# Turning the kept blocks one step earlier, and moving the side tasks into the fresh unit's split

## The chip, the cores and the metric

The kernel runs on one core of one Trainium2 chip. The metric is the device time of one execution in microseconds (us). TensorE is written PE (PEld is its weight load), VectorE DVE, ScalarE ACT; SP is SyncE, which here issues nearly all DMAs. The kernel before took 2707.97 us (median of three runs, 2707.35 to 2708.66).

## What is computed

Three layers follow each other over 4 batches of 3072 rows with 256 columns (12288 rows in all). The reference, cut to its core:

```python
scores = np.matmul(z, z.transpose(0, 2, 1)) / S      # z: 4 x 3072 x 64, symmetric scores
x = u * np.matmul(np.maximum(scores, 0.0) ** 2, v)   # attention without softmax
h = x @ w_in                                         # 256 -> 2048
x = (h - np.tanh(h)) @ w_out                         # 2048 -> 256
xk = mu_k * x + (1 - mu_k) * x_prev                  # x_prev: the row above, zero at a batch's start
xr = mu_r * x + (1 - mu_r) * x_prev
k = np.maximum(xk @ w_k, 0.0)                        # 256 -> 1024
out = 1 / (1 + np.exp(-(xr @ w_r))) * ((k * k) @ w_v)
```

Weights arrive in float64 and are made float32 in the kernel.

## The kernel before

**Tiles.** Rows are cut into 24 tiles of 512 (`t` or `i`), six (`NG`) to a batch; `g = t % 6` is a tile's place in its batch. Everything is held transposed, with columns on the partitions and 512 rows along the free dimension. Each product is made of three matmuls (`PASSES`): each operand is split into a high part (`h`) and the rest (`l`), and high by high, high by low and low by high are summed. So every intermediate goes from PSUM through an ACT function, is copied to `h` and has `l = a - h` taken from it on DVE (`sub_lo`, line 96) before PE can use it.

**Units.** The work is a list of 504 units, `units`, which the loop at line 702 takes one by one as `n`. A unit's `produce` issues its first matmuls and its split, and `consume` of the unit two places back (`LAG` = 2) issues the matmuls that add it to the accumulator. A unit `A` (12 for each of 24 tiles) is a 256 x 512 block of the squared scores, `H` (8 a tile) a 256-column slice of the tanh layer, `K` (4) one of the squared layer, `R` (1) the sigmoid. All `A` units come first; behind them `H` of a tile is interleaved with `K` and `R` of the tile before.

**Fresh and re-read units.** Scores are symmetric, so a block of tile pair (i, g) that was made for tile i is, transposed, also a block for tile g. In tiles g = 1 to 5, blocks of source tiles i below `min(g, 3)` (`AGAIN` = 3) are not made again: they were stored to DRAM when fresh (`keep`), are loaded as tiles `b` by SP seven units ahead (`again_load`) and turned by DVE (line 401). A fresh unit has 4 + 12 matmuls, and ACT does relu (line 339), square (340) and, for g above 1, the copy to `h` (93). A re-read unit has 12 matmuls alone; DVE does two transposes, ACT the copy to `h_t` (93), DVE `l_t` (96). `pairs[g]` sets the order of a tile's units. For g = 3 to 5 it is re-read, fresh, re-read, fresh and so on, six of each.

**Order.** Engines run their instructions in the order in which the code is written; nothing is rearranged. For unit n the loop runs: DMA loads due (`loads`), the store of the unit before, `produce(n)`, `consume(n - 2)`, `turned_high(n + 1)` (if unit n+1 is re-read: its two transposes and the copy to `h_t`), and `run_steps(n)`. When a re-read unit is produced, only `l_t` is left to do. `run_steps` places side tasks: the z, v, u and weight preparation of later tiles, the product with `u` that ends a tile (`x1_steps`), and in the last stage the mixing with the row above (`mix_steps`) and the output. Each has a first place, a last place and a cost per step. A unit has a budget (line 677 to 680: 1.4 for A with g up to 1; 2.1 for fresh and 0.1 for re-read units with g above 1; 2.2 for H, 2.4 K, 4.0 R), and up to 1.0 of an unused budget is carried to the next unit (`spare`, line 689), as is any overdraft.

**Buffers.** Score and tanh results have two PSUM tiles (`wk`), accumulators two (`acc`), `h` and `l` three each, ACT's results (`a_`, `t_`, `g_`) four (`scratch`), the re-read blocks share twelve with v and the weights.

Of the kernel before, what the change touches and what calls it, by code (L numbers as in the profile page):

```python
# [19 lines left out]
def relu2_attention__tanh_ffn__channel_mix_kernel(  # L20
# [25 lines left out]
    nc = tc.nc  # L46
# [6 lines left out]
    NT = B * NG  # L53
# [4 lines left out]
    LAG = 2  # L58
# [33 lines left out]
    def copy_hi(o, i):  # L92
        nc.scalar.activation(out=o, in_=i, func=ACTF.Copy)  # L93
# [232 lines left out]
    def parts(name):  # L326
        h = sb.tile([P, 2, 512], F32R, tag="hi", name=f"h_{name}", bufs=3)
        l = sb.tile([P, 2, 512], F32R, tag="lo", name=f"l_{name}", bufs=3)
        return h, l
# [1 line left out]
    def scratch(name):  # L331
        return sb.tile([P, 2, 512], F32, tag="e", name=name, bufs=4)

    def square_split(name, w, sc, pieces=1, high=nc.vector.tensor_copy):
        a = scratch(f"a_{name}")
        h, l = parts(name)
        for j in range(pieces):
            x = slice(2 * j // pieces, 2 * (j + 1) // pieces)
            nc.scalar.activation(out=a[:, x], in_=w[:, x], func=ACTF.Relu, scale=sc)  # L339
            nc.scalar.activation(out=a[:, x], in_=a[:, x], func=ACTF.Square)  # L340
            high(h[:, x], a[:, x])  # L341
            sub_lo(l[:, x], a[:, x], h[:, x])
        return a, h, l
# [5 lines left out]
    for g in range(NG):  # L349
        of_f = [2 * j + h for j in fresh[g] for h in range(2)]  # L350
        of_r = [2 * j + h for j in again[g] for h in range(2)]
        if g == 1:
            of_f = of_f[2:] + of_f[:2]
        if len(of_r) == 2:
            pairs[g] = of_f[:8] + [of_r[0], of_f[8], of_r[1], of_f[9]]
        elif len(of_r) == 4:
            pairs[g] = [x for i in range(4) for x in (*of_f[2 * i : 2 * i + 2], of_r[i])]
        elif of_r:
            pairs[g] = [x for i in range(6) for x in (of_r[i], of_f[i])]
        else:  # L360
            pairs[g] = of_f
    kept = {(b, i, g): dr.tile([TB, TB], F32, name=f"at{b}_{i}_{g}")
# [18 lines left out]
        g, q = n // NP % NG, n % NP  # L381
        return pairs[g][q] // 2 in again[g]

    def turned_high(n):
        if not is_again(n):
            return
        t, q = divmod(n, NP)
        b, g = divmod(t, NG)
        kp = pairs[g][q]
        x = blocks[b, g, kp // 2]  # L390
        a = scratch(f"t_{t}_{q}")
        h, l = parts(f"t_{t}_{q}")
        for j in range(2):
            f = kp % 2 * 2 + j
            y = x[:, :, f * 32 : f * 32 + 32]
            if g < AGAIN:
                y = y.rearrange("p (c k) i -> p k c i", c=4)
                o = a[:, j].rearrange("p (k c i) -> p k c i", k=4, c=4)
            else:
                o = a[:, j].rearrange("p (m i) -> p m i", i=32)  # L400
            nc.vector.transpose(out=o, in_=y)  # L401
        copy_hi(h, a)
        turned[n] = (a, h, l)

    def produce(unit):
        kind, t, p = unit
        name = f"{kind}{t}_{p}"
        n = at[unit]
        if n in turned:
            a, h, l = turned.pop(n)  # L410
            sub_lo(l, a, h)
            split[unit] = (h, l)
            return
        w = work(f"w_{name}")
        if kind == "A":
            b, g = divmod(t, NG)
            kp = pairs[g][p]
            for j in range(2):
                kc = 2 * kp + j
                lhsT = z1[b, kc // 4][:, (kc % 4) * P : (kc % 4 + 1) * P]  # L420
                nc.tensor.matmul(w[:, j], lhsT, zq[b, g], start=True, stop=False)  # L421
                nc.tensor.matmul(w[:, j], lhsT, z2[t], start=False, stop=True)  # L422
            a, *split[unit] = square_split(
                name, w, scale, 2 if t == 0 and p == 0 else 1,
                copy_hi if g > 1 else nc.vector.tensor_copy,
            )
            if (b, g, kp // 2) in kept:
                stores[n + 1] = lambda: keep(b, g, kp, a)
        elif kind in ("H", "K"):
            wt = "in" if kind == "H" else "k"  # L430
            x = xs[t] if kind == "H" else mixed["k", t]
            for j in range(2):
                f = 2 * p + j
                n = 0
                for c in range(DC):
                    for a, m in PASSES:
                        nc.tensor.matmul(  # L437
                            w[:, j],
                            ws[wt, f // 4][a][:, c, (f % 4) * P : (f % 4 + 1) * P],
                            x[m][:, c],  # L440
                            start=n == 0,
                            stop=n == 3 * DC - 1,
                        )
                        n += 1
            if kind == "K":
                _, *split[unit] = square_split(name, w, 1.0)
            else:
                g = scratch(f"g_{name}")
                h, l = parts(name)
                nc.scalar.activation(out=g, in_=w, func=ACTF.Tanh)  # L450
                nc.vector.tensor_tensor(out=g, in0=w, in1=g, op=ALU.subtract)  # L451
                copy_hi(h, g)
                sub_lo(l, g, h)
                split[unit] = (h, l)
        elif kind == "R":
            x = mixed["r", t]
            for d in range(DC):
                n = 0
                for c in range(DC):
                    for a, m in PASSES:  # L460
                        nc.tensor.matmul(  # L461
                            w[:, d],
                            ws["r", 0][a][:, c, d * P : (d + 1) * P],
                            x[m][:, c],
                            start=n == 0,
                            stop=n == 3 * DC - 1,
                        )
                        n += 1
            s = p4(f"sg{t}")
            nc.scalar.activation(out=s, in_=w, func=ACTF.Sigmoid)  # L470
            split[unit] = s
# [135 lines left out]
    def task(first, last, steps, *args):  # L607
        tasks.append([last, first, len(tasks), steps, args])
# [9 lines left out]
    for t in range(NT):  # L618
        load(t * NP - NP + 1 if t > 1 else 5 + 3 * t, u_load, t)
        task(t * NP - 6 if t > 1 else 8 + 3 * t, t * NP + NP - 2, u_steps, t)  # L620
        if t:
            load(t * NP - 3, z_swap, t)
        task(t * NP + NP + LAG - 1, t * NP + NP + LAG + 3, x1_steps, t)
    for b in range(1, B):
        prev = (b - 1) * NG * NP
        last = prev + (NG - 1) * NP
# [43 lines left out]
    def run_steps(n):  # L670

        for x in [x for x in tasks if x[1] <= n]:
            tasks.remove(x)
            ready.append((x[0], list(x[3](*x[4]))))
        ready.sort(key=lambda x: x[0])
        kind = units[min(n, len(units) - 1)][0]
        left = {"A": 1.4, "H": 2.2, "K": 2.4, "R": 4.0}[kind]
        if kind == "A" and n // NP % NG > 1:
            left = 0.1 if is_again(n) else 2.1
        left += spare[0]  # L680
        while ready and (left > 0 or ready[0][0] <= n):
            for x in list(ready):
                if left > 0 or x[0] <= n:
                    cost, f = x[1].pop(0)
                    f()
                    left -= cost
                    if not x[1]:
                        ready.remove(x)
        spare[0] = min(left, 1.0)

    with tc.manual_schedule():
        z_load(0, 0)
        z_load(0, 1)
        v_load(0, 0)
        z_load(0, 2)
        v_load(0, 1)
        for cost, f in z_steps(0, 0) + z_steps(0, 1) + v_steps(0, 0):
            f()
        for m, src in ((0, moe2_mu_k), (1, moe2_mu_r)):
            with nc.allow_non_contiguous_dma(reason="a column of the mixing vector"):  # L700
                nc.sync.dma_start(out=mu[:, m, :], in_=src.rearrange("(c p) -> p c", p=P))
        for n in range(len(units) + LAG + 3):
            for f in loads.pop(n, ()):
                f()
            if n in stores:
                stores.pop(n)()
            if n < len(units):
                produce(units[n])
            if LAG <= n < len(units) + LAG:
                consume(units[n - LAG])  # L710
            turned_high(n + 1)
            if n == 1:
                nc.vector.memset(zero, 0.0)
                nc.vector.tensor_scalar(
                    out=omu, in0=mu, scalar1=-1.0, scalar2=1.0, op0=ALU.mult, op1=ALU.add
                )
            run_steps(n)
        assert not loads and not tasks and not ready


# [27 lines left out]
```

## Time and profile before

| | us |
|---|---|
| median of the runs | 2707.97 |
| the profiled execution | 2708.13 |
| its span, first to last instruction | 2706.3 |
| first matmul of A, of H, last matmul starts | 6.64, 1043.70, 2697.98 |
| PE busy, share of the span | 2631.3 (97%) |
| PE weight loads busy | 2144.3 (79%) |
| DVE, ACT busy | 1674.3 (62%), 1385.7 (51%) |
| matmuls | 11424 |

All matmuls have 128 x 128 weights and 512 moving columns. The profile counts a matmul as busy from its start to its modelled end, so busy times of neighbours overlap; how close PE is to its pace is read from the starts of matmuls. Work on DVE and ACT costs time only where PE, directly or through them, waits for it.

### The profile page before, as it was taken

To read this page: it belongs to the slowest core of one execution; us is meant where nothing else is said; L and a number is where in the kernel's file an instruction comes from. 1 tells how busy PE (TensorE), PEld (TensorE's weight loads), DVE (VectorE), ACT (ScalarE), POOL (GpSimd) and SP (SyncE) were. 2 spreads that over 40 slices of the span, in tenths; PEclk is the share of its full clock that TensorE was granted. 3 is DMA by queue.
4 is the path that set the end of the run, shared out by engine and by line. 5 is a ranking of instruction groups with operands and counts; after the bars stand their busy time and mean duration, and the time that the engine had idled before them with its cause. 6 is when DMAs were issued, how large, how long until landed. Compare 5 with 4: busy or idle time off the path is not lost.

```text
span 2706.3 us, 28503 instructions
## 1 busy us (share of the span) xinstructions
PE 2631.3 (97%) x11424; PEld 2144.3 (79%) x11424; DVE 1674.3 (62%) x1880; ACT 1385.7 (51%) x1502; POOL 0.2 (0%) x4
## 2 busy tenths in 40 slices
PE   8999999999899999999999999999999999999998
PEld 6877877787678777888888888888888888888887
DVE  7777877787777556555555555555555555555554
ACT  6656665656566665444444444444444444444443
POOL 0000000000000000000000000000000000000000
PEclk9999999999999999999999999999999999999999
DMA  8675576577557642000000000000000000000000
GB/s 224 185 185 131 185 206 146 129 222 206 125 132 219 165 98 87 9 16 16 16 16 16 16 16 16 16 16 16 16 16 16 16 16 16 16 16 16 16 8 16
DMA packets 415604, 203.99 MB, mean 75 GB/s; under 512 B 261488, under 2 KB 372080, under 8 KB 415472
## 3 DMA queue, kind: packets, MB, share of 16 engines
q1 hardware_dynamic: 414416, 202.04, 29.3%
q8 instruction: 89, 1.46, 0.2%
q14 instruction: 43, 0.35, 0.0%
q10 hardware_dynamic: 1056, 0.13, 0.0%
HBM read 114.03 MB, written 82.05 MB: 72 GB/s over the span
## 4 chain that ended last, share of the span: by engine, by line
PE 68%; ACT 12%; DVE 11%; issue 4%; DMA 3%; SPq 2%; ACTq 0%; DVEq 0%
PE acc_H L493 19%; PE w_H L437 15%; PE acc_A L493 11%; PE w_K L437 10%; PE acc_K L493 7%; DVE t L401 3%; PE w_R L461 2%; ACT a_A L340 2%; ACT h_A L93 2%; ACT a_A L339 2%; DVE l_A L96 2%; DMA b<-at 2%; PE w_A L422 2%; PE w_A L421 2%; ACT h_t L93 1%
## 5 line engine op out<-in xcount | busy, mean ns | idle before, releaser
L437 PE MATMUL w_H<-xh,w_in 128*128 128x512 f32 x1536 | 507.0, 391 | 10.1 <-DVE g_H L451 10.1
L493 PE MATMUL acc_A<-h_A,v 128*128 128x512 f32 x1536 | 503.6, 390 | 2.0 <-ACT h_A L93 1.4
L493 PE MATMUL acc_H<-h_H,w_out 128*128 128x512 f32 x1536 | 504.2, 389 | 0.0
L93 ACT ACTIVATE h_H<-g_H 128x1024 fp32r<-128x1024 f32 x192 | 203.7, 1061 | 395.0 <-DVE g_H L451 395.0
L96 DVE TENSOR_TENSOR l_H<-g_H,h_H 128x1024 fp32r<-128x1024 f32 x192 | 235.3, 1225 | 216.3 <-ACT h_H L93 216.3
L437 PEld LDWEIGHTS w_H<-xh,w_in 128*128 128x128 f32 x1536 | 288.3, 188 | 79.2 <-DVE g_H L451 19.3
L451 DVE TENSOR_TENSOR g_H<-w_H,g_H 128x1024 f32<-128x1024 f32 x192 | 233.2, 1215 | 172.1 <-ACT g_H L450 172.1
L493 PEld LDWEIGHTS acc_A<-h_A,v 128*128 128x128 f32 x1536 | 288.8, 188 | 63.3 <-ACT h_A L93 2.6
L96 DVE TENSOR_TENSOR l_A<-a_A,h_A 128x1024 fp32r<-128x1024 f32 (+1 forms) x193 | 235.3, 1219 | 167.1 <-ACT h_A L93 158.4
L493 PEld LDWEIGHTS acc_H<-h_H,w_out 128*128 128x128 f32 x1536 | 288.3, 188 | 59.9
L450 ACT ACTIVATE g_H<-w_H 128x1024 f32<-128x1024 f32 x192 | 195.3, 1017 | 237.3 <-PE w_H L437 237.2
L493 PE MATMUL acc_A<-l_A,v 128*128 128x512 f32 x768 | 301.5, 393 | 4.6 <-DVE l_A L96 3.7
L437 PE MATMUL w_H<-x,w_in 128*128 128x512 f32 x768 | 299.3, 390 | 0.0
L493 PE MATMUL acc_H<-l_H,w_out 128*128 128x512 f32 x768 | 298.8, 389 | 0.0
L493 PE MATMUL acc_A<-h_t,v 128*128 128x512 f32 x768 | 257.7, 398 | 0.0
L339 ACT ACTIVATE a_A<-w_A 128x1024 f32<-128x1024 f32 (+1 forms) x193 | 195.6, 1014 | 110.4 <-PE w_A L422 93.1
L437 PE MATMUL w_K<-mkh,w_k 128*128 128x512 f32 x768 | 251.9, 389 | 0.0
L493 PE MATMUL acc_K<-h_K,w_v 128*128 128x512 f32 x768 | 251.9, 389 | 0.0
L93 ACT ACTIVATE h_t<-t 128x1024 fp32r<-128x1024 f32 x96 | 101.9, 1062 | 259.7 <-DVE t L401 235.6
L341 DVE CAST h_K<-a_K 128x1024 fp32r<-128x1024 f32 x96 | 66.6, 694 | 229.3 <-ACT a_K L340 229.3
L340 ACT ACTIVATE a_A<-a_A 128x1024 f32<-128x1024 f32 (+1 forms) x193 | 203.9, 1056 | 6.1
L493 PE MATMUL acc_A<-l_t,v 128*128 128x512 f32 x384 | 158.8, 414 | 41.9 <-DVE l_t L96 40.5
(127 smaller groups left out, 3486.2 us busy)
## 6 DMA issues: line engine op xcount, KB each, us to landing
at<-a_A SPq DMA_DIRECT2D x96, 512.0 KB, 4.7
b<-at SPq DMA_DIRECT2D x192, 256.0 KB, 5.0
vr<-in_v_dram SPq DMA_DIRECT2D x24, 512.0 KB, 5.5
uin<-in_u_dram SPq DMA_DIRECT2D x192, 64.0 KB, 2.6
x1d<-x SPq DMA_DIRECT2D x24, 512.0 KB, 3.1
x<-x1d SPq DMA_DIRECT2D x24, 512.0 KB, 3.7
out_dram<-ot SPq DMA_DIRECT2D x192, 64.0 KB, 1.9
zin<-in_z_dram SPq DMA_DIRECT2D x94, 64.0 KB, 3.6
```

Of the source, the lines that this page charges most:

```text
L93: nc.scalar.activation(out=o, in_=i, func=ACTF.Copy)
L96: nc.vector.tensor_tensor(out=o, in0=i, in1=hi.bitcast(F32), op=ALU.subtract)
L339: nc.scalar.activation(out=a[:, x], in_=w[:, x], func=ACTF.Relu, scale=sc)
L340: nc.scalar.activation(out=a[:, x], in_=a[:, x], func=ACTF.Square)
L341: high(h[:, x], a[:, x])
L401: nc.vector.transpose(out=o, in_=y)
L421: nc.tensor.matmul(w[:, j], lhsT, zq[b, g], start=True, stop=False)
L422: nc.tensor.matmul(w[:, j], lhsT, z2[t], start=False, stop=True)
L437: nc.tensor.matmul(w[:, j], ws[wt, f // 4][a][:, c, (f % 4) * P : (f % 4 + 1) * P], x[m][:, c], start=n == 0, stop=n == 3 * DC - 1,)
L450: nc.scalar.activation(out=g, in_=w, func=ACTF.Tanh)
L451: nc.vector.tensor_tensor(out=g, in0=w, in1=g, op=ALU.subtract)
L493: nc.tensor.matmul(o[:, c], w[a][:, c * P : (c + 1) * P], s[m][:, j], start=p == 0 and j == 0 and n == 0, stop=p == last and j == 1 and n ...
```

## The change

Three functions and a few lines change. (1) `turned_high` is split. `turn(n + 1)`, with the two transposes, is called at the start of `produce` of a fresh unit n, ahead of that unit's matmuls and split; `turned_high(n + 1)`, now the copy to `h_t` alone, stays behind `consume`. (2) In a fresh unit the side tasks are no longer placed behind the unit: `square_split` calls `run_steps(n)` through `beside`, between ACT's square and the copy to `h`. Re-read units and all units behind the A units still call it at the end. (3) For g = 3 to 5 the units of a tile now alternate fresh, re-read. (4) An unused budget is no longer carried over (`spare` is at most 0); overdrafts still are. (5) `x1_steps` has its first place one unit later.

```diff
@@ square_split
-    def square_split(name, w, sc, pieces=1, high=nc.vector.tensor_copy):
+    def square_split(name, w, sc, pieces=1, high=nc.vector.tensor_copy, beside=None):
...
             nc.scalar.activation(out=a[:, x], in_=a[:, x], func=ACTF.Square)
+            if j == 0 and beside:
+                beside()
             high(h[:, x], a[:, x])
...
-            pairs[g] = [x for i in range(6) for x in (of_r[i], of_f[i])]
+            pairs[g] = [x for i in range(6) for x in (of_f[i], of_r[i])]
...
-    def turned_high(n):
+    def turn(n):
...
         a = scratch(f"t_{t}_{q}")
-        h, l = parts(f"t_{t}_{q}")
...
             nc.vector.transpose(out=o, in_=y)
-        copy_hi(h, a)
-        turned[n] = (a, h, l)
+        turned[n] = a
+
+    def turned_high(n):
+        if n in turned:
+            h, l = parts("t_{}_{}".format(*divmod(n, NP)))
+            copy_hi(h, turned[n])
+            turned[n] = (turned[n], h, l)
...
         if kind == "A":
+            turn(n + 1)
...
-                copy_hi if g > 1 else nc.vector.tensor_copy,
+                copy_hi if g > 1 else nc.vector.tensor_copy, lambda: run_steps(n),
...
-        task(t * NP + NP + LAG - 1, t * NP + NP + LAG + 3, x1_steps, t)
+        task(t * NP + NP + LAG, t * NP + NP + LAG + 3, x1_steps, t)
...
-        spare[0] = min(left, 1.0)
+        spare[0] = min(left, 0.0)
...
-            run_steps(n)
+            if n >= NT * NP or is_again(n):
+                run_steps(n)
```

What this does to the order, at three places. In names, `A16_6` is unit 6 of tile 16, `b2_4_1` the block of batch 2, tile place 4, source 1; the number at the end only counts tiles.

**DVE in tile 16 (g = 4), before:** `cw_` and `v3_1` are side tasks.

```order
L96 TENSOR_TENSOR l_A16_5_5761<-a_A16_5_5759,h_A16_5_5760 128x1024
L401 STREAM_TRANSPOSE t_16_6_5778<-b2_4_1_5527 128x512 x2
L96 TENSOR_TENSOR v3_1_5729<-vr3_1_5623,v3_1_5729 128x1024
L249 TENSOR_TENSOR cw_v1_0_5612<-cw_v1_0_5612 128x512
L250 TENSOR_SCALAR cw_v1_0_5612<-cw_v1_0_5612 128x512
L96 TENSOR_TENSOR l_t_16_6_5780<-t_16_6_5778,h_t_16_6_5779 128x1024
L96 TENSOR_TENSOR l_A16_7_5807<-a_A16_7_5805,h_A16_7_5806 128x1024
L401 STREAM_TRANSPOSE t_16_8_5824<-b2_4_2_5647 128x512 x2
```

and now:

```order
L96 TENSOR_TENSOR l_t_16_5_5753<-t_16_5_5722,h_t_16_5_5752 128x1024
L402 STREAM_TRANSPOSE t_16_7_5774<-b2_4_1_5548 128x512 x2
L96 TENSOR_TENSOR v3_1_5734<-vr3_1_5606,v3_1_5734 128x1024
L255 SCALAR_TENSOR_TENSOR cw_v1_0_5621<-c_v1_0_5491,cw_v1_0_5621 128x512
L258 TENSOR_TENSOR cw_v1_0_5621<-cw_v1_0_5621 128x512
L96 TENSOR_TENSOR l_A16_6_5783<-a_A16_6_5781,h_A16_6_5782 128x1024
L96 TENSOR_TENSOR l_t_16_7_5806<-t_16_7_5774,h_t_16_7_5805 128x1024
L402 STREAM_TRANSPOSE t_16_9_5822<-b2_4_2_5664 128x512 x2
```

The transposes of a re-read unit stood behind `l` of the fresh unit ahead of it; now they stand ahead of that, with the side tasks between.

**DVE where tile 8's H units begin, before:** `mk`/`mr` are the mixing of tile 7, `o` and `ot` the output of tile 6, `g_H` the tanh result less its argument.

```order
L543 CAST mkh7_11552<-mxk7_11538 128x1024
L543 CAST mrh7_11554<-mxr7_11542 128x1024
L96 TENSOR_TENSOR mkl7_11556<-mxk7_11538,mkh7_11552 128x1024
L451 TENSOR_TENSOR g_H8_0_11571<-w_H8_0_11558,g_H8_0_11571 128x1024
L96 TENSOR_TENSOR l_H8_0_11573<-g_H8_0_11571,h_H8_0_11572 128x1024
L559 TENSOR_TENSOR o6_11590<-acc_K6_11363,sg6_11520 128x512
L96 TENSOR_TENSOR mrl7_11592<-mxr7_11542,mrh7_11554 128x1024
L451 TENSOR_TENSOR g_H8_1_11607<-w_H8_1_11594,g_H8_1_11607 128x1024
L96 TENSOR_TENSOR l_H8_1_11609<-g_H8_1_11607,h_H8_1_11608 128x1024
L569 STREAM_TRANSPOSE ot6_11614<-o6_11590 128x512
L559 TENSOR_TENSOR o6_11590<-acc_K6_11363,sg6_11520 128x512
L451 TENSOR_TENSOR g_H8_2_11634<-w_H8_2_11621,g_H8_2_11634 128x1024
```

and now:

```order
L550 CAST mkh7_11552<-mxk7_11538 128x1024
L458 TENSOR_TENSOR g_H8_0_11567<-w_H8_0_11554,g_H8_0_11567 128x1024
L96 TENSOR_TENSOR l_H8_0_11569<-g_H8_0_11567,h_H8_0_11568 128x1024
L566 TENSOR_TENSOR o6_11586<-acc_K6_11363,sg6_11520 128x512
L96 TENSOR_TENSOR mkl7_11588<-mxk7_11538,mkh7_11552 128x1024
L458 TENSOR_TENSOR g_H8_1_11603<-w_H8_1_11590,g_H8_1_11603 128x1024
L96 TENSOR_TENSOR l_H8_1_11605<-g_H8_1_11603,h_H8_1_11604 128x1024
L576 STREAM_TRANSPOSE ot6_11610<-o6_11586 128x512
L550 CAST mrh7_11616<-mxr7_11542 128x1024
L566 TENSOR_TENSOR o6_11586<-acc_K6_11363,sg6_11520 128x512
L96 TENSOR_TENSOR mrl7_11619<-mxr7_11542,mrh7_11616 128x1024
L458 TENSOR_TENSOR g_H8_2_11634<-w_H8_2_11621,g_H8_2_11634 128x1024
```

`mrh7` and `mkl7` went from ahead of `g_H8_0` to behind it, and the same instructions in all still stand ahead of `g_H8_2`. The other tiles have the same rows at this place.

**DVE at the program's start, before:** `zt0_2` and `z1_0_2` prepare the third z tile.

```order
L96 TENSOR_TENSOR v0_0_174<-vr0_0_148,v0_0_174 128x1024
L341 CAST h_A0_0_187<-a_A0_0_186 128x512
L96 TENSOR_TENSOR l_A0_0_188<-a_A0_0_186,h_A0_0_187 128x512
L341 CAST h_A0_0_187<-a_A0_0_186 128x512
L96 TENSOR_TENSOR l_A0_0_188<-a_A0_0_186,h_A0_0_187 128x512
L118 STREAM_TRANSPOSE zt0_2_197<-zin0_2_150 128x512
```

and now:

```order
L96 TENSOR_TENSOR v0_0_174<-vr0_0_148,v0_0_174 128x1024
L118 STREAM_TRANSPOSE zt0_2_191<-zin0_2_150 128x512
L119 CAST z1_0_2_192<-zt0_2_191 128x512
L96 TENSOR_TENSOR z1_0_2_192<-zt0_2_191,z1_0_2_192 64x512
L343 CAST h_A0_0_187<-a_A0_0_186 128x512
L96 TENSOR_TENSOR l_A0_0_188<-a_A0_0_186,h_A0_0_187 128x512
```

The z steps stand ahead of the first unit's split, and ACT's copy of that z tile stands ahead of the second half of its relu.

## Rows read from the trace of the kernel before

**Rows 1.** Windows: elapsed us, then each engine's busy us (count), clock, DMA share, GB/s

```profile
1045.00:1155.00 110.00, 110.00 (x487) 91.07 (x487) 64.35 (x58) 54.45 (x59) 0.00 (x0) 1.00 0.06 20
6.60:52.40 45.80, 42.55 (x168) 33.55 (x169) 38.23 (x51) 32.34 (x35) 0.00 (x0) 1.00 0.84 222
52.40:1043.70 991.30, 944.17 (x4033) 756.59 (x4032) 740.08 (x932) 605.98 (x594) 0.00 (x0) 0.99 0.64 168
139.20:268.40 129.20, 117.50 (x493) 92.23 (x492) 98.19 (x128) 77.44 (x78) 0.00 (x0) 0.99 0.69 158
...
920.10:1043.70 123.60, 118.40 (x493) 92.15 (x492) 75.21 (x81) 76.33 (x75) 0.00 (x0) 0.99 0.48 121
1043.70:2698.00 1654.30, 1644.25 (x7225) 1354.11 (x7223) 890.79 (x892) 745.48 (x872) 0.00 (x0) 1.00 0.07 16
```

**Rows 2.** Waits of PE, whole span: us in total, times, longest

```profile
PE acc_A L493 <- DVE l_t L96: 40.5, 33, 3.5
PE w_H L437 <- DVE g_H L451: 10.1, 22, 0.5
```

**Rows 3.** Timeline of ACT and DVE, tile 22 (g = 4): start, us, instruction, idle before

```profile
982.88 1.06 ACT L93 ACTIVATE h_t<-t 128x1024 fp32r<-128x1024 f32 x1 [2.56 <-DVE t L401]
...
989.61 1.06 ACT L93 ACTIVATE h_t<-t 128x1024 fp32r<-128x1024 f32 x1 [2.57 <-DVE t L401]
...
991.61 1.06 ACT L340 ACTIVATE a_A<-a_A 128x1024 f32<-128x1024 f32 x1
992.71 1.06 ACT L93 ACTIVATE h_A<-a_A 128x1024 fp32r<-128x1024 f32 x1
...
987.07 1.23 DVE L96 TENSOR_TENSOR l_A<-a_A,h_A 128x1024 fp32r<-128x1024 f32 x1 [0.72 <-ACT h_A L93]
988.22 1.30 DVE L401 STREAM_TRANSPOSE t<-b 128x512 f32<-128x512 f32 x2
990.70 1.22 DVE L96 TENSOR_TENSOR l_t<-t,h_t 128x1024 fp32r<-128x1024 f32 x1 [1.19 <-ACT h_t L93]
```

**Rows 4.** Tile 16: PE's longest wait there (timeline), and a window right behind it

```profile
711.77 0.56 PE L493 MATMUL acc_A<-l_t,v 128*128 128x512 f32 x1 [2.65 <-DVE l_t L96]
...
712.10:715.40 3.30, 3.30 (x9) 2.60 (x8) 1.16 (x2) 2.08 (x2) 0.00 (x0) 0.50 0.70 129
```

**Rows 5.** Timeline of ACT, DVE and PE where tile 8's H units begin

```profile
1574.94 1.01 ACT L450 ACTIVATE g_H<-w_H 128x1024 f32<-128x1024 f32 x1
...
1576.35 0.69 DVE L543 CAST mrh<-mxr 128x1024 fp32r<-128x1024 f32 x1
...
1578.09 1.22 DVE L451 TENSOR_TENSOR g_H<-w_H,g_H 128x1024 f32<-128x1024 f32 x1
...
1587.99 1.21 DVE L451 TENSOR_TENSOR g_H<-w_H,g_H 128x1024 f32<-128x1024 f32 x1
...
1579.36 0.50 PE L437 MATMUL w_H<-xh,w_in 128*128 128x512 f32 x1 [0.46 <-DVE g_H L451]
...
1590.41 0.39 PE L437 MATMUL w_H<-xh,w_in 128*128 128x512 f32 x1
```

**Rows 6.** Block b2_4_1: its load's landing (page), SP's issues, DVE's first use (timelines)

```profile
b<-at SPq DMA_DIRECT2D x192, 256.0 KB, 5.0
...
698.11 2.83 SPq L375 DMA_DIRECT2D b<-at  x4
...
722.11 1.30 DVE L401 STREAM_TRANSPOSE t<-b 128x512 f32<-128x512 f32 x2
```

**Rows 7.** Timeline of PE and DVE at the program's start

```profile
12.46 0.79 PE L421 MATMUL w_A<-zq,z 128*128 128x512 f32 x1 [1.81 <-ACT a_A L339]
...
19.52 0.50 PE L493 MATMUL acc_A<-h_A,v 128*128 128x512 f32 x1 [0.63 <-DVE h_A L341]
...
14.18 0.70 DVE L118 STREAM_TRANSPOSE zt<-zin 128x512 f32<-128x512 f32 x1
...
15.38 0.69 DVE L96 TENSOR_TENSOR z<-zt,z 64x512 fp32r<-64x512 f32 x1
```

## The prediction

> **What bounds the kernel now.** First the windows. In a full flow 487 matmuls start in 110.00 us, 226.3 ns apart [rows 1]; over longer such stretches it is 226.5 ns, which I use. 11424 of them make 2587 us of the 2708.13 of the profiled execution, so PE's flow is the bound and the rest is interruptions. What a stretch loses is its elapsed time less its matmuls, less one, times 0.2265 us [rows 1]: the start 45.80 - 167 x 0.2265 = 8.0; attention behind it 991.30 - 4032 x 0.2265 = 78.0; the last stage 1654.30 - 7224 x 0.2265 = 18.1. The stretches of tiles g = 3 to 5 lose 17.8 in the first batch and 12.2 in the last; the four together, by the same working, 68 of the 78.
>
> PE's idle gaps alone say less: attention 991.30 - 944.17 = 47.1, the last stage 10.05 [rows 1], 57 where the starts say 96. The Trainium skill ("Perfetto Trace Analysis", Identifying the Most-Contended Engine) says of matmul busy share that it is no good measure of how close TensorE is to its best, since pipelined matmuls look smaller; these rows agree. A sum by idle gaps would end at 2651 or above; mine doesn't use it.
>
> Next PE's waits: 33 for `l_t`, up to 3.5 us, and 22 short ones of `w_H` for `g_H` [rows 2]. Last the timelines at these places.
>
> **Attention.** Before, a pair (re-read, fresh) is a closed loop through DVE and ACT: `l_A` of the fresh unit, two transposes behind it, the copy to `h_t`, relu, square, `h_A`, and the next `l_A`. `h_t` waits for the transposes, `l_A` for `h_A`, and `h_t` comes every 989.61 - 982.88 = 6.73 us [rows 3], where PE needs 28 x 0.2265 = 6.34. The loop costs 0.39 a pair; 18 pairs in each of four batches make 28 us. The other 40 in these stretches and 10 elsewhere come from side tasks, which stand inside the loop between transposes and `l_t`, and from the clock: behind a wait of 2.65 us, PE's granted clock is 0.50 (1.2 GHz) for 3.30 us, in which 9 matmuls start instead of 14.6 [rows 4].
>
> After, the transposes stand ahead of the fresh split and need only a loaded block, so the loop is open. I lay out a pair at PE's pace with the durations of [rows 3], 0 being the fresh unit's first matmul: relu 1.1, square 2.1, `h_A` 3.2, `h_t` 4.2 on ACT; on DVE the next transposes until 1.5, `l_A` 4.3 to 5.6, `l_t` 5.5 to 6.7. The accumulation reads `l_A` at 33 x 0.2265 = 7.5 and `l_t` at 45 x 0.2265 = 10.2: slack 1.9 and 3.5. Work on ACT is 4.2 of 6.34. Between transposes and `l_A` DVE has 2.8 us free, and 4.7 before PE waits. The heaviest unit of the new order puts two z steps there, 2 x 1.89 by [rows 7] = 3.8, within 4.7. Units that have ACT copies as well (seven with one, two with two) come out at stalls of 0.2 to 0.3, some 2 in all; I leave 4 to be lost, since the layout resolves tenths and the pairs are many. Gain 78 - 4 = 74. The bounds are 53 (0.26 us lost in each of 96 pairs, all re-read units) and 78. [...] Side tasks bring their DMA issues along; on SP these change places with the stores of blocks, behind which nothing is waited for within the leads below.
>
> **Last stage.** 18.1 over 22 tiles is 0.8 each, at `w_H` of unit 2, which waits for `g_H` of unit 0 [rows 5]. The tanh is done at 1574.94 + 1.01 = 1575.95, but DVE first does `mrh` and `mkl`, from 1576.35 to 1578.09. Without the carried budget these stand behind; `g_H8_0` starts at 1576.35, 1.74 earlier, more than the 0.8. What is late next: the same work is ahead of `g_H8_2`, so that still ends at 1587.99 + 1.21 = 1589.20, while its reader comes 0.79 earlier than 1590.41, at 1589.62, its weights up to one matmul before, 1589.40. So 0.1 to 0.2 is left. A margin that small is the weakest step here. Gain 22 x 0.79 = 17.4; bounds 17.4 and, if the wait passes to unit 4, 0.
>
> **Start.** The z steps now stand ahead of the first split, and ACT's copy of that tile ahead of the second half of relu, for which PE already waits 1.81 at 12.46 [rows 7]. The z takes 15.38 + 0.69 - 14.18 = 1.89, so that matmul comes up to 2.5 us later with the copy. Against that the next unit's relu and split come about 1 us earlier, and PE waits for that split at 19.52 [rows 7]. I take +1.1, bounds 0 and 3. Here a rule speaks against the change. By the trace a long wait is followed by clock 0.50 [rows 4]. The Trainium skill ("TensorE: Matmul & The Clock Gate", Part 1: The HAM clock gate) says that the throttled state is the default and that activity releases it. By it the release at the start comes later too; an estimate from the row at 0.50, some 6 matmuls by 0.2 us, would make the start +2.3 and the time 2619. It is within my bounds.
>
> **Sum.** 2708.13 - 74 - 17.4 + 1.1 = 2617.8. The median stood 0.16 below the profiled execution, so 2618.
>
> **Rivals.** (1) The stall of the last stage stays, moved to unit 4 or still behind the same DVE work. For: the margin of 0.1 to 0.2. Against: even if late by 0.1 it costs 22 x 0.1 = 2, and only a second DVE instruction in front costs all. 2618 + 17 = 2635. (2) The wait moves from `l_t` to `l_A`: the loop's 28 us go, but side tasks now delay the fresh split, whose slack (1.9) is less than that of `l_t` (3.5). For: on DVE they now stand ahead of `l_A` in every fresh unit. Against: the heaviest fits. All of the other 50 kept gives 2618 + 46 = 2664, half of it 2641. (3) Slower: with the transposes at the head of DVE ahead of the fresh split, a block that isn't there stops the fresh units too. DVE has 4.7 us before PE waits, and the gain of 90 is used up at 90 / 48 blocks = 1.9 us more, so from 6.6 us late on the kernel is slower; 7 us late gives 2618 + 48 x 2.3 = 2728. Against: block b2_4_1 was issued by 700.94 and first used at 722.11, a lead of 21.2, about 18 with the new place, while landing takes 5.0 [rows 6]. (4) It doesn't do what it says: another wait sets the pair's 6.73 and the 0.8, and it stays at 2709. Against: at both places the rows name the releaser, and it is one the change moves.
>
> **How the numbers follow.** Forecast 0.71 (2611 to 2630), rival 1 0.10, rival 2 0.13, rival 3 0.03, rival 4 0.03. About 0.2% (5.4 us) is what a measurement of this kernel can tell from no change. Faster is the first three, 0.94; same 0.03; slower 0.03. The range 2610 to 2645 holds forecast, rival 1 and the milder part of rival 2, about 0.87; its lower end is the sum with all of 78 gained and nothing lost at the start: 2708.13 - 78 - 17.4 = 2612.7, less 2 for the pace, which the windows give to about 0.1%.
>
> **What would show it.** The pair of g = 3 to 5 at 6.34 instead of 6.73, no `l_t` waits and no window below clock 1.00 in attention; `h_t` of ACT not waiting for transposes; H's first matmul near 970 instead of 1043.70. In the last stage no `w_H` waits and 7225 matmuls in about 1637 us. At the start the wait of [rows 7] longer by 2 or so and the loss of that stretch 9 instead of 8. I would be wrong if PE waits for `l_A` where side tasks stand ahead of it, if a `g_H` wait turns up at unit 4, or if DVE's transposes wait for a DMA.

## The result and the profile after

The changed kernel takes 2616.78 us (median of four runs, 2616.64 to 2617.14) against 2707.84 before: a ratio of 0.9664, interval 0.9647 to 0.968. The prediction was 2618, range 2610 to 2645. The profiled execution took 2616.88, its span is 2615.1.

First the windows, in the columns of [rows 1] and by its stages: start, attention, tiles g = 3 to 5 of the last batch, last stage.

```profile
6.70:53.90 47.20, 42.40 (x168) 34.25 (x169) 39.73 (x53) 32.59 (x36) 0.00 (x0) 0.93 0.83 220
53.90:969.45 915.55, 915.50 (x4033) 756.28 (x4033) 732.77 (x929) 605.88 (x595) 0.00 (x0) 1.00 0.69 181
855.20:969.40 114.20, 114.20 (x505) 94.58 (x504) 72.29 (x80) 76.72 (x76) 0.00 (x0) 1.00 0.54 133
969.45:2606.80 1637.35, 1637.35 (x7225) 1355.67 (x7223) 891.75 (x893) 747.54 (x871) 0.00 (x0) 1.00 0.07 16
```

Attention now takes 915.55 us for the 4033 matmuls that took 991.30, with the clock at 1.00 throughout. 915.55 - 4032 x 0.2265 = 2.3 us is lost there, where it was 78. The last stage takes 1637.35 where it took 1654.30.

PE's waits over the whole span, in the form of [rows 2]. The first two, both at the start, are all that is left of the matmuls' own. In attention only the weight load (PEld) still waits, five times, for `l_A`:

```profile
PE w_A L428 <- ACT zq L93: 6.8, 1, 6.8
PE w_A L428 <- ACT a_A L339: 4.7, 1, 4.7
PEld acc_A L500 <- DVE l_A L96: 2.1, 5, 0.5
```

The same pair of tile 22 as in [rows 3], timeline of PE, ACT and DVE (start, us, instruction, idle before):

```profile
899.64 0.39 PE L428 MATMUL w_A<-z,z 128*128 128x512 f32 x1
907.12 0.39 PE L500 MATMUL acc_A<-l_A,v 128*128 128x512 f32 x1
...
900.74 1.03 ACT L339 ACTIVATE a_A<-w_A 128x1024 f32<-128x1024 f32 x1 [2.19 <-PE w_A L429]
...
903.86 1.04 ACT L93 ACTIVATE h_t<-t 128x1024 fp32r<-128x1024 f32 x1
907.09 1.03 ACT L339 ACTIVATE a_A<-w_A 128x1024 f32<-128x1024 f32 x1 [2.19 <-PE w_A L429]
...
899.92 1.30 DVE L402 STREAM_TRANSPOSE t<-b 128x512 f32<-128x512 f32 x2
903.99 1.23 DVE L96 TENSOR_TENSOR l_A<-a_A,h_A 128x1024 fp32r<-128x1024 f32 x1 [1.66 <-ACT h_A L93]
905.13 1.22 DVE L96 TENSOR_TENSOR l_t<-t,h_t 128x1024 fp32r<-128x1024 f32 x1
```

Relu comes every 907.09 - 900.74 = 6.35 us, PE's own pace, and now waits for PE's `w_A`. `h_t` no longer waits for the transposes, which are done 2.6 us before it starts. `l_A` is ready at 905.22 and read at 907.12: the slack of 1.9 that the prediction laid out.

The place of [rows 5], DVE and PE in tile 8:

```profile
1497.46 1.22 DVE L458 TENSOR_TENSOR g_H<-w_H,g_H 128x1024 f32<-128x1024 f32 x1
...
1509.09 1.22 DVE L458 TENSOR_TENSOR g_H<-w_H,g_H 128x1024 f32<-128x1024 f32 x1
...
1499.62 0.62 PE L444 MATMUL w_H<-xh,w_in 128*128 128x512 f32 x2
...
1510.73 0.39 PE L444 MATMUL w_H<-xh,w_in 128*128 128x512 f32 x1
```

`g_H8_0` ends at 1498.68 and `w_H8_2` (the second of the two matmuls from 1499.62) has no wait. `g_H8_2` ends at 1510.31, 0.42 ahead of its reader.

And the start, PE and a window behind its wait, then PE in the kernel before, behind the wait of [rows 7]:

```profile
15.19 0.79 PE L428 MATMUL w_A<-zq,z 128*128 128x512 f32 x1 [4.72 <-ACT a_A L339]
...
15.10:19.60 4.50, 4.41 (x10) 3.47 (x11) 2.01 (x4) 4.44 (x6) 0.00 (x0) 0.50 0.67 160
...
13.05 0.63 PE L422 MATMUL w_A<-z,z 128*128 128x512 f32 x1
13.48 0.63 PE L421 MATMUL w_A<-zq,z 128*128 128x512 f32 x1
```

The wait of 1.81 in [rows 7] became 4.72, and behind it the granted clock is 0.50 (1.2 GHz): 10 matmuls in 4.50 us, 0.43 us apart. Behind its shorter wait the kernel before had them 0.43 apart too (13.05, 13.48), until 15.61; in the changed kernel this lasts until 20.05.

### The profile page after: what moved, and what is told of

The parts are those of the page before. It is cut to its first block, busy times and chain, and to the rows that moved or that the text cites. A ratio compares the mean times of both kernels' runs of the same rounds, so it can differ in the third digit from the quotient of the medians.

```text
span 2615.1 us, 28460 instructions
## 1 busy us (share of the span) xinstructions
PE 2595.5 (99%) x11424; PEld 2146.2 (82%) x11424; DVE 1669.4 (64%) x1880; ACT 1387.9 (53%) x1502; POOL 0.2 (0%) x4
## 4 chain that ended last, share of the span: by engine, by line
PE 99%; DVE 1%; ACT 0%; DMA 0%; issue 0%; ACTq 0%; DVEq 0%
PE acc_A L500 30%; PE acc_H L500 20%; PE w_H L444 20%; PE acc_K L500 10%; PE w_K L444 10%; PE w_A L428 3%; PE w_A L429 3%; PE w_R L468 2%; DVE z L96 0%; DMA zin<-in_z_dram 0%; DVE zt L118 0%; ACT zq L93 0%; DVE l_A L96 0%; ACT h_A L93 0%; DVE z L119 0%
## 5 line engine op out<-in xcount | busy, mean ns | idle before, releaser
L444 PE MATMUL w_H<-xh,w_in 128*128 128x512 f32 x1536 | 500.4, 389 | 0.0
L500 PE MATMUL acc_A<-h_t,v 128*128 128x512 f32 x768 | 252.0, 389 | 0.0
L339 ACT ACTIVATE a_K<-w_K 128x1024 f32<-128x1024 f32 x96 | 98.8, 1029 | 136.8 <-PE w_K L444 134.5
L500 PEld LDWEIGHTS acc_A<-l_A,v 128*128 128x128 f32 x768 | 144.6, 188 | 32.3 <-DVE l_A L96 2.1
```

The lines of the kernel that those rows point to most:

```text
L444: nc.tensor.matmul(w[:, j], ws[wt, f // 4][a][:, c, (f % 4) * P : (f % 4 + 1) * P], x[m][:, c], start=n == 0, stop=n == 3 * DC - 1,)
L500: nc.tensor.matmul(o[:, c], w[a][:, c * P : (c + 1) * P], s[m][:, j], start=p == 0 and j == 0 and n == 0, stop=p == last and j == 1 and n ...
```

## The experiments

Each kernel's lost time is its matmul starts less 0.2265 us a matmul, cut at the first matmul of tile 1 and of H (cuts elsewhere, as in [rows 1], move it by some 0.3). Times in us.

| kernel | time | lost: start | attention | last stage |
|---|---|---|---|---|
| before | 2707.84 | 7.7 | 78.0 | 18.3 |
| changed | 2616.78 | 9.1 | 2.3 | 1.2 |
| spare_only | 2690.78 | 9.3 | 77.4 | 1.2 |
| spare_back | 2635.26 | 9.0 | 3.7 | 18.2 |
| turn_back | 2681.59 | 9.0 | 67.2 | 1.2 |
| turn_only | 2644.22 | 7.7 | 13.1 | 18.2 |
| sides_end | 2615.13 | 7.8 | 1.8 | 1.2 |
| order_back | 2617.85 | 9.0 | 3.4 | 1.2 |
| dve_more_065 | 2626.08 | 9.1 | 11.6 | 1.2 |
| dve_more_130 | 2656.54 | 9.1 | 41.7 | 1.2 |
| late_g2 | 2618.85 | 9.0 | 2.2 | 3.5 |
| load_late | 2636.82 | 9.0 | 21.6 | 1.2 |
| load_late_sides_end | 2648.36 | 7.7 | 33.8 | 1.2 |
| start_late_v | 2615.25 | 7.2 | 1.8 | 1.2 |

The kernel before gave medians of 2707.8 to 2708.9 beside these, so differences of about 1 us between rows are read from the lost times, not from the medians. `spare_only` loses 9.3 at the start, where its engines have the same order as in the kernel before: there the granted clock is 0.50 once more, from 20.90 to 24.30.

### The carried budget: spare_only, spare_back

In the kernel before, and in the changed one the other way round:

```diff
-        spare[0] = min(left, 1.0)
+        spare[0] = min(left, 0.0)
```

> The kernel before with one line changed: an unused budget of side tasks lapses. Theory (the last stage's 22 stalls come from the carried budget alone, the attention's from the order around the transposes): the last stage loses 1 instead of 18, attention stays within 10 of its 78, so 2708 - 17 = 2691 (2680 to 2701). Rival (the carried budget also piles up the side tasks that delay l_t in attention): most of the 40 to 50 that side tasks cost there goes too, 2640 to 2660.

> The changed kernel with the carried budget put back. Theory: the last stage's 22 waits of w_H for g_H come back, +17, and attention keeps its gain, since up to 1.0 more of side tasks still fits into the 4.7 us of room ahead of l_A nearly everywhere: 2634 (2632 to 2640). Rival (the lapse is needed in attention as well): 2645 or more, with waits for l_A there.

Both came out as the theory had it: 2690.78 and 2635.26. Alone, the lapse takes the last stage from 18.3 to 1.2 and leaves attention at 77.4. Put back, it brings 18.2 back with the same row of PE's waits as in [rows 2], and leaves attention at 3.7:

```profile
PE w_H L444 <- DVE g_H L458: 10.1, 22, 0.5
```

The last stage's gain is the lapse's alone, and the gain in attention doesn't need the lapse beside the rest of the change.

### The place of the transposes: turn_back, turn_only

`turn_back` is the changed kernel with

```diff
-            turn(n + 1)
...
+            turn(n + 1)
             turned_high(n + 1)
```

so that the transposes stand behind the fresh split again. `turn_only` is the kernel before with the changed kernel's `turn` and `turned_high`, and

```diff
             split[unit] = (h, l)
+            turn(n + 1)
             return
...
         if kind == "A":
+            turn(n + 1)
```

(the first of the two lines because a tile of g = 3 to 5 starts with a re-read unit there, behind another).

> The changed kernel with the transposes put back behind the split of the fresh unit; side tasks, order of units and lapse as changed. Theory (the closed loop l_A, transposes, h_t, relu, square, h_A, l_A sets 6.73 us a pair): the loop comes back, 72 x 0.39 = 28, and side tasks above some 1.9 us on DVE lengthen it: 2645 to 2665, h_t waiting for the transposes in g = 3 to 5. Rival (the place of the side tasks or the order of units made the gain): within 5 of 2617.

> The kernel before with one part of the change alone: the two transposes of a re-read unit stand ahead of the matmuls and split of the unit before it. Side tasks, order of units and carried budget are those of before. Theory (the open loop alone makes the gain in attention): attention loses 2 to 8 instead of 78, the last stage keeps its 18, the start its 8: 2634 to 2642. Rival (the other parts are needed too, since with the transposes behind the split the gain was only 27): 2660 or more.

`turn_back` lost more than expected, 67.2 in attention. The loop is there as before, at 6.72 us a pair. Tile 22, ACT and DVE:

```profile
980.04 1.06 ACT L93 ACTIVATE h_t<-t 128x1024 fp32r<-128x1024 f32 x1 [2.56 <-DVE t L402]
...
986.76 1.06 ACT L93 ACTIVATE h_t<-t 128x1024 fp32r<-128x1024 f32 x1 [2.57 <-DVE t L402]
...
985.37 1.30 DVE L402 STREAM_TRANSPOSE t<-b 128x512 f32<-128x512 f32 x2
```

Pairs without side tasks in the last batch lose 0.35 to 0.43 each, as counted. But I had given side tasks 1.9 us of free room in the loop. Of the pairs with them many lose no more than that, others 0.5 to 2.3, and those in which ACT's copy `zq` stands mostly 3 to 4. Three times the clock is at 0.50 for 3.4 us (from 246.9, 461.9 and 506.3), though no single wait of PE in attention is longer than 1.1 us. Side tasks that stand between square and `h_A` are inside this loop on both engines. PE then waits for three different tiles:

```profile
PE acc_A L499 <- DVE l_t L96: 14.1, 28, 0.6
PE acc_A L499 <- DVE l_A L96: 10.2, 16, 1.0
PE acc_A L499 <- ACT h_A L93: 6.8, 7, 1.1
```

`turn_only` shows the other side: this one move takes attention from 78.0 to 13.1 with everything else as before. The theory had 2 to 8 there and 2634 to 2642 in all; it came to 2644.22, nearer to it than to the rival's 2660. Of the 13, 9.5 are lost in tiles g = 1 and 2 of three batches, where the kernel before lost its "10 elsewhere" too:

```profile
126.10 0.50 PE L501 MATMUL acc_A<-l_A,v 128*128 128x512 f32 x1 [0.74 <-DVE l_A L96]
...
119.60 1.24 DVE L188 STREAM_TRANSPOSE uT<-uin 128x1024 f32<-128x1024 f32 x1
...
123.31 0.42 DVE L243 TENSOR_SCALAR cw_out<-cw_out 128x512 int32<-128x512 int32 x1
```

From 119.60 to 123.7 DVE has side tasks in one pile (`uT` and six steps of a weight), and the transposes and `l_A` come behind it. In the other kernels with the transposes ahead and the normal loads, at most 0.2 is lost in these tiles. So neither the carried budget alone (`spare_back`) nor side tasks behind the units alone (`sides_end`, below) brings that loss; whether it takes both, or the earlier first place of `x1_steps`, was not separated.

### The place of the side tasks and the order of units: sides_end, order_back

`sides_end` calls the side tasks behind every unit again:

```diff
-                copy_hi if g > 1 else nc.vector.tensor_copy, lambda: run_steps(n),
+                copy_hi if g > 1 else nc.vector.tensor_copy,
...
-            if n >= NT * NP or is_again(n):
-                run_steps(n)
+            run_steps(n)
```

`order_back` is the changed kernel with

```diff
-            pairs[g] = [x for i in range(6) for x in (of_f[i], of_r[i])]
+            pairs[g] = [x for i in range(6) for x in (of_r[i], of_f[i])]
...
             split[unit] = (h, l)
+            turn(n + 1)
             return
```

> The changed kernel with the side tasks behind every unit again, transposes ahead. Theory (the open loop is the gain; side tasks then stand between l_A and l_t, and l_t has 3.5 us of slack): only the heaviest units stall, 2617 to 2632. Rival (the place of the side tasks made the other half of the gain): 2640 to 2664.

> The changed kernel with the units of g = 3 to 5 in the order re-read, fresh again (the first re-read unit of such a tile, which then follows another re-read unit, is turned ahead of that one). Theory (the order of units is only what lets the transposes stand ahead; the open loop does the rest): within 5 of the changed kernel, 2615 to 2622. Rival (the alternation itself makes the gain): 2630 or more, with waits for l_t or l_A in g = 3 to 5.

Neither part is needed by itself; `turn_only`, which has neither, nor the lapse and the later `x1_steps`, loses 13.1. `sides_end` came out below the range I gave. With the side tasks at the end attention loses 1.8, where the changed kernel loses 2.3, and the start is better, since `z` steps and their ACT copy are behind the first split again:

```profile
12.50 0.80 PE L428 MATMUL w_A<-zq,z 128*128 128x512 f32 x1 [1.82 <-ACT a_A L339]
```

So by the lost times `sides_end` is ahead by the 1.35 us of the start (9.12 against 7.77) and the small difference in attention. The runs alone don't show it: its 2615.13 and the changed kernel's 2616.78 were taken at different times, and their ratios to before (0.9655, interval 0.9627 to 0.9683, and 0.9664) overlap. The order of units costs or gives about 1 us.

### How much room is left: dve_more_065, dve_more_130

```diff
-            nc.vector.transpose(out=o, in_=y)
+            for _ in range(1 + (j == 0 and g > 2)):
+                nc.vector.transpose(out=o, in_=y)
```

and in the second run `range(1 + (g > 2))`: one or both transposes of tiles g = 3 to 5 are done twice.

> The changed kernel with the first transpose of each re-read unit of g = 3 to 5 done twice, 0.65 us more of DVE ahead of the fresh unit's split in each of 72 pairs. Theory (DVE is busy 5.36 of 6.34 us a pair in the first three batches, 4.02 in the last, and has 4.7 us of room ahead of l_A, of which the heaviest unit uses 3.8): it still fits but for a few units with copies on ACT, 2617 to 2623. Rival (the changed kernel stands at the edge): 0.65 x 54 = 35 more, 2650.

> As the run with 0.65 us, with both transposes done twice, 1.30 us more a pair. Theory: DVE then has 5.36 + 1.30 = 6.66 us of work for a pair of 6.34 in the first three batches and becomes the bound there, 54 x 0.32 = 17, with some clock drops behind the waits: 2633 to 2655; the last batch, 4.02 + 1.30 = 5.32, keeps its 114.1 us for tiles g = 3 to 5. Rival (the room ahead of l_A and not the sum decides): the last batch loses as well.

2626.08 and 2656.54, both above what I gave. The tiles g = 3 to 5 took, by batch, 114.9, 114.6, 114.9, 114.2 us in the changed kernel; 118.3, 118.5, 116.8, 114.2 with 0.65 more; 128.8, 128.8, 126.3, 114.2 with 1.30 more. The last batch, which has few side tasks, loses nothing even with 1.30, so neither the bare loop nor the sum of DVE's work is near its limit there. In the others the sum would cost 18 x 0.32 = 5.8 a batch; it cost 11 to 14. The loss is at some 20 units, most of them with heavy side tasks; with 1.30 PE's waits are

```profile
PE acc_A L501 <- ACT h_A L93: 12.8, 8, 2.1
PE acc_A L501 <- DVE l_A L96: 12.1, 16, 1.4
```

Unit A4_4, which lost 0.3 in the changed kernel already, shows why (that kernel's DVE and ACT):

```profile
190.33 0.69 DVE L96 TENSOR_TENSOR z<-zt,z 64x512 fp32r<-64x512 f32 x1
192.66 1.23 DVE L96 TENSOR_TENSOR l_A<-a_A,h_A 128x1024 fp32r<-128x1024 f32 x1 [1.65 <-ACT h_A L93]
...
191.05 0.63 ACT L93 ACTIVATE zq<-z 128x512 fp32r<-128x512 f32 x1 [0.55 <-DVE z L96]
191.59 1.04 ACT L93 ACTIVATE h_A<-a_A 128x1024 fp32r<-128x1024 f32 x1
```

ACT's copy `zq` waits for the last of DVE's z steps, `h_A` stands behind that copy on ACT, and `l_A` waits for `h_A`. So here the side tasks are on the path twice, and 0.65 more ahead of them costs 0.65 at once (this unit's loss went from 0.3 to 1.1). The room of 4.7 holds for side tasks on DVE alone.

### The margin in the last stage: late_g2

```diff
+                if p == 2:
+                    nc.vector.tensor_copy(out=l[:, 0], in_=x[0][:, 0])
                 nc.vector.tensor_tensor(out=g, in0=w, in1=g, op=ALU.subtract)
```

> The changed kernel with one more DVE copy of 0.43 us ahead of the subtraction of each tile's H unit 2. The trace of the changed kernel shows g_H8_2 ending at 1510.31 and its reader at 1510.73. Theory (of these 0.42 some 0.2 to 0.3 are the weight load and the signal, as predicted): 22 tiles lose 0.2 to 0.3 each, 2621 to 2624, with waits of w_H for g_H at unit 4. Rival (the whole 0.42 is free): 2617.

2618.85; the last stage loses 3.5 instead of 1.2, which is 0.1 a tile. It is lost at unit 4, where the weight load now waits in all 22 tiles. That wait (whole span), then DVE and PE in tile 8:

```profile
PEld w_H L444 <- DVE g_H L460: 5.1, 22, 0.2
...
1509.37 0.42 DVE L459 CAST l_H<-xh 128x512 fp32r<-128x512 f32 x1
1509.70 1.22 DVE L460 TENSOR_TENSOR g_H<-w_H,g_H 128x1024 f32<-128x1024 f32 x1
...
1511.01 0.47 PE L444 MATMUL w_H<-xh,w_in 128*128 128x512 f32 x1
```

The added copy moves `g_H` by 1509.70 - 1509.37 = 0.33, since it overlaps its neighbour, not by its 0.42. 0.33 less the 0.1 that was lost leaves 0.22 to 0.23 of margin. The expected loss of 0.2 to 0.3 was the longer copy less a margin that I took at its lower end.

### When a block is late: load_late, load_late_sides_end

```diff
-            load(t * NP + pairs[g].index(2 * i) - 7, again_load, b, g, i)
+            load(t * NP + pairs[g].index(2 * i) - 3, again_load, b, g, i)
```

in the changed kernel, then in `sides_end`.

> The changed kernel with the blocks' loads placed three units ahead instead of seven. The changed kernel's leads from the last issue to the first transpose are 15 to 30 us; four units are 12.7 us, so 2 to 17 are left, and landing takes about 5. Theory (a late block stops DVE at the transposes but has 4.7 us of room before PE waits): some of the 48 blocks come up to 3 us late, DVE waits for a DMA there, PE hardly: 2617 to 2622. Rival (a block that is late stops the fresh unit's split and PE by as much): 10 to 20 blocks by 1 to 3 us, 2635 to 2660.

> The run sides_end with the loads three units ahead, as in load_late. There three blocks came 4.9 to 7.2 us late and PE then waited 3.5 to 4.9 for l_A, since 3.3 us of side tasks stood between the late transposes and l_A. Theory (the room is 4.7 us less the side tasks in between): with the side tasks behind l_A the same lateness costs PE 0 to 2.5 a block and no clock drop: 2616 to 2624. Rival (a late block costs its lateness wherever the side tasks stand): 2633 or more.

Both totals were missed: 2636.82 and 2648.36, the second worse than the first. Tile 5, unit 8, in `load_late`: DVE, then PE, then SP's issue of that block:

```profile
242.85 1.30 DVE L402 STREAM_TRANSPOSE t<-b 128x512 f32<-128x512 f32 x2 [5.05 <-DMA b<-at]
...
247.35 1.22 DVE L96 TENSOR_TENSOR l_A<-a_A,h_A 128x1024 fp32r<-128x1024 f32 x1
...
248.63 0.79 PE L500 MATMUL acc_A<-l_A,v 128*128 128x512 f32 x1 [3.49 <-DVE l_A L96]
...
231.02 3.97 SPq L377 DMA_DIRECT2D b<-at  x4
```

and in `load_late_sides_end`:

```profile
248.55 1.31 DVE L402 STREAM_TRANSPOSE t<-b 128x512 f32<-128x512 f32 x2 [6.28 <-DMA b<-at]
249.78 1.18 DVE L96 TENSOR_TENSOR l_A<-a_A,h_A 128x1024 fp32r<-128x1024 f32 x1
...
251.02 0.51 PE L500 MATMUL acc_A<-l_A,v 128*128 128x512 f32 x1 [4.31 <-DVE l_A L96]
...
236.80 4.59 SPq L377 DMA_DIRECT2D b<-at  x4
```

What I had wrong is when the block comes. The load's four parts were issued within 231.02 to 234.99 and used at 242.85, 7.9 us later; landing, counted from a part's issue, took up to 10.0 in these two runs, where the medians are 4.9 and 5.2. With the side tasks at the end, SP issued the same block later: the unit's first matmul is at 237.50 in the one and 238.96 in the other, the issue 6.5 and 2.2 us ahead of it. The trace names the cause. SP issues its loads in the order of the code, and `zin` loads precede the block's. They wait until DVE's step `zt`, a side task, has read the `zin` tile whose buffer they take:

```profile
227.31 0.70 DVE L118 STREAM_TRANSPOSE zt<-zin 128x512 f32<-128x512 f32 x1
228.04 1.91 SPq L108 DMA_DIRECT2D zin<-in_z_dram  x4
...
233.09 0.70 DVE L118 STREAM_TRANSPOSE zt<-zin 128x512 f32<-128x512 f32 x1
233.83 1.91 SPq L108 DMA_DIRECT2D zin<-in_z_dram  x4
```

The first two lines are of `load_late`, the others of `load_late_sides_end`. Against the unit's first matmul that is 9.5 and 5.1 us ahead: with `zt` placed later, the loads behind it are issued later, here by 4.3, and my theory had the lateness unchanged.

What I had right is the price. From the unit's first matmul, the transposes start at 5.35 and at 9.59, and `l_A` is ready at 11.07 and 12.00: with side tasks in between 5.7 later, without 2.4. Over all blocks of tiles g = 3 to 5 for which DVE waited in these two runs, PE is on time whenever transposes, side tasks and `l_A` end by 7.4 (four of the eight waits of `load_late`, of 0.76 to 1.95 us, cost nothing), and otherwise late by the excess: transposes at 5.51 with nothing in between, `l_A` ready at 7.92 and read at 7.97 instead of 7.48. That is the room of 4.7 less the side tasks in between.

### The start: start_late_v

```diff
-        for cost, f in z_steps(0, 0) + z_steps(0, 1) + v_steps(0, 0):
+        late = v_steps(0, 0)
+        for cost, f in z_steps(0, 0) + z_steps(0, 1, late):
...
                 produce(units[n])
+            if n == 0:
+                for cost, f in late:
+                    f()
```

in `sides_end`; `late` also takes the `zq` copy of that z tile.

> The kernel of the run sides_end (side tasks behind every unit) with v's first preparation and ACT's copy of the second z tile moved behind the first unit's split at the program's start. In sides_end the fifth pair of first-layer matmuls waits 1.8 us for a relu that stands behind these two copies on ACT. Theory: that wait goes, and part of it comes back at the first accumulation, which needs v's low part: 2612.5 to 2614.5 against 2615.1. Rival (the start is bound by the lower clock and the loads): 2615.

2615.25 (2614.42 to 2616.00). The start loses 7.2 instead of 7.8: the wait of 1.8 is gone, and waits of 0.65 for v's low part (at 13.80) and 0.82 for a later unit's relu (at 17.18) came in its place; one for `h_A` (0.52, now 0.62) stayed. No gain that these runs resolve.

## Why the prediction was right

**The pace and the sum.** 226.5 ns a matmul held: the changed kernel runs its last stage at it to 1.2 us in 1637. By terms: attention 78.0 - 2.3 = 75.8 gained (74 foreseen), last stage 18.3 - 1.2 = 17.1 (17.4), start 1.4 lost and a first matmul 0.14 later (1.1). 2708.13 - 75.8 - 17.1 + 1.5 = 2616.7; the profiled execution took 2616.88. Counting idle gaps instead of starts would have missed it by over 30.

**The open loop.** This step carried the prediction, and `turn_only` and `turn_back` isolate it: 65 of the 76 with the transposes' place alone, 11 with all the rest and without it. `l_A` and `l_t` ready 5.6 and 6.7 after the unit's first matmul were laid out to a tenth (899.64, 905.22, 906.35).

**The small stalls.** Foreseen: some 2 us in nine units with copies on ACT. Found: five of these with 0.3 each (A4_4, A5_4, A11_4, A15_10, A16_10), none elsewhere. The 4 that I left for what the layout can't resolve was 2 too much.

**The last stage.** The 22 stalls went and did not move to unit 4. The margin that I called the weakest step, 0.1 to 0.2, is 0.22 by `late_g2`.

**The start.** +1.4 against +1.1 is in part luck, since the terms were off both ways. The matmul behind the wait came 2.7 us later, not up to 2.5 (the wait grew by 2.9); the longer stretch at half pace behind it made the fourth unit 3.5 us later than before (21.29 against 17.75); and the next split gave back 2.0, not 1, since PE's waits of 0.63 (19.52) and 0.76 (20.78) in the kernel before are gone. That leaves 1.5, with the first matmul's 0.14. The +2.3 that the rule on the clock gave did not come. In `late_g2`, with the same start, the clock is back at 1.00 from 18.0 instead of 20.2, but then a weight load waits 0.75 for DVE at 21.75, and the start loses 9.0 instead of 9.1: so the later release explains 0.1 of it. The Trainium skill ("TensorE: Matmul & The Clock Gate", Part 1: The HAM clock gate) has the throttled state as the default; the window at 0.50 behind the wait agrees.

**The rivals.** (1) did not come, and one more DVE instruction ahead of `g_H8_2`, 0.33 us, costs only 2. (2) fails by `sides_end`: with the rest of the change in place, attention loses about 2 us wherever the side tasks stand. It is not far off, though: 0.65 us more a pair costs 9. My view of before, that 40 to 50 us were the side tasks' own doing, was loose: they cost that only inside the closed loop, as `turn_back` shows with side tasks at the new place. (3) is real as a mechanism, but its room of 4.7 holds only with no side tasks behind the transposes; with 3.3 of them it is 1.4. Its lead of 18 was compared with a median landing of 5.0; landings under load took up to 10, and four units less lead, 12.7 us, were enough to lose 20. And the prediction let the loads on SP change places only with stores; they also stand behind `zin` loads that wait for DVE. The margin was thinner than the prediction says. (4) is out: the pair takes 6.35 us, and both releasers are gone.

## What to carry to other kernels

Where an engine that should be the bound idles a little in every round, look for a closed loop through the other engines, and find the operation in it that needs nothing from the round: moving that one ahead (here two transposes) was worth more than all placing of side work. Judge lost time by the starts of instructions against the pace of an undisturbed stretch, since busy times of pipelined instructions hide part of it. A margin for a transfer is its lead less its longest landing beside the traffic at that place, not its median; and a side task that moves can move the loads that stand behind its own.

## What the runs showed of the hardware

The clock of a row can be one that nobody recorded. The changed kernel's trace has no record of the granted clock before 10.0 us, and a window counts such time as 1.00. What PE did is then read from its starts, 0.43 apart as in the window at 0.50:

```profile
8.00:10.00 2.00, 2.00 (x6) 1.59 (x5) 1.24 (x3) 0.66 (x2) 0.00 (x0) 1.00 0.97 137
...
8.45 0.63 PE L429 MATMUL w_A<-z,z 128*128 128x512 f32 x1
8.88 0.63 PE L428 MATMUL w_A<-zq,z 128*128 128x512 f32 x1
```

The start's row in [rows 1], at 1.00, has such a stretch too: the records of the kernel before begin at 15.7, and until 15.61 its matmuls start 0.43 apart, from 15.91 on 0.23.

A DVE instruction of 0.42 us delays what follows by 0.33, as neighbours overlap; added work is costed by differences of starts.
